# SyncE's list: a weight load that gave way to a transpose looks again from its new place

## The chip, the cores and the metric

The kernel runs on one core of one Trainium2 chip. The metric is the device time of one execution in microseconds (us); shorter is better. The core has five engines that run side by side: TensorE (PE in the profile), VectorE (DVE), ScalarE (ACT), GpSimd (POOL) and SyncE (SP). SyncE computes nothing here; it issues every transfer of the kernel, loads as well as transposes, one after the other in the order of one fixed list.

## The reference

Four residual layers on a sequence of 2048 rows of 576 numbers in bf16: attention, MLP, attention, MLP, with the same two sets of weights used twice.

```python
def _A_ref(x, wqkv, wo):                       # 32 heads of 18, window W = 256
    qkv = (x @ wqkv).reshape(B, S, 3, H, Dh)...
    scores = einsum("bhqd,bhkd->bhqk", q, k) * (Dh ** -0.5)
    mask = (idx[:, None] - idx[None, :] >= 0) & (idx[:, None] - idx[None, :] < W)
    p = softmax(where(mask, scores, -1e9))
    o = einsum("bhqk,bhkd->bhqd", p, v)
    return o... @ wo
def _B_ref(x, w1, b1, w2, b2):                 # 576 -> 4608 -> 576
    y = _layernorm(x)
    h = gelu(einsum("bsd,df->bsf", y, w1) + b1)
    return einsum("bsf,fd->bsd", h, w2) + b2
x = A_x
x = x + _A_ref(_layernorm(x), A_wqkv, A_wo)
x = x + _B_ref(_layernorm(x), B_w1, B_b1, B_w2, B_b2)
x = x + _A_ref(_layernorm(x), A_wqkv, A_wo)
x = x + _B_ref(_layernorm(x), B_w1, B_b1, B_w2, B_b2)
```

## The kernel before

**Tiles and chunks.** The rows are cut into 16 tiles of 128, and four tiles make a chunk of 512 rows. With two layers there are eight chunks, k = 0 to 7. The attention of chunk k runs interleaved with the MLP of chunk k - 1, so that TensorE has matmuls while ScalarE does exponentials.

**Stages.** Each task carries the name of its stage. For the attention of chunk k: `q{k}` makes queries, keys and values (matmuls at L855, for chunk 1 at L799), `ea{k}`, `eb{k}`, `ec{k}` are scores, exponentials, masks and the product with the values (L922, L933, L954, L975), `t{k}` is the output projection with its residual, statistics and normalization (L796, L1031, L711, L736). For the MLP: `ga`, `gb`, `gc` are the three thirds of the first matmul with its Gelu (L1088, L1098), and `ma`, `mb`, `mc` the three thirds of the second (L796 and L799, residual at L1031). `ln{k}` normalizes the rows for the queries of chunk k.

**Transposes.** Matmuls need their inputs with the contracted dimension on the partitions. So normalized rows `xn` are transposed by a transfer into `xnTa` (for the attention) or `xnTm` (for the MLP), at L759, and queries and keys `qn` into `qT` and `kT`, at L895. Both are issued by SyncE. Before an `xn` tile is transposed, GpSimd copies its last 64 columns (L744). For odd chunks each transpose into `xnTm` also names the buffers `kx0` and `kx1` as written, so that it waits for the one before it to land.

**Weight loads.** The weights of the MLP do not stay in the on-chip memory; they are streamed from HBM for each chunk. `w1` comes in six blocks per chunk into three slots; one block is three transfers, one of 768 KB and two of 48 KB. Two blocks are asked for in each of `ga`, `gb` and `gc`, always for a stage later on. `w2` comes in thirds into one buffer of two halves, two transfers of 864 KB each. All are issued at L648 (`dma`) and appear as `w_sb<-in_B_w_dram`; a load waits until the matmuls that read the buffer's old content are done. In the task's field `dma` they are "w1" and "w2", and a transpose is "t".

**The planner.** `Plan.schedule` plays the whole program through with an estimated cost for each task. It repeatedly takes the task that can start earliest, with priorities and nudges by stage as tie-breaks. The result, `order`, is the list of tasks with planned start times `st`, and each engine executes its part of the list in that order; the order is fixed when the kernel is built, and what each task waits for is worked out from what it reads and writes. A task's `ready` is the planned time at which its data are there.

**The pass that the change touches.** After the plan is made, a last pass shifts some weight loads back in the list. `turns` holds the planned start and the ready time of every transpose. A load of w1 or w2 that is planned at `st` gets the new place `at`, just behind the last transpose that starts less than 4 us after `st` and has its data at most `YIELD` = 3 us after `st`. Only loads planned from `YIELD_FROM` on are looked at. Whatever depends on a load is kept behind it through `first`. Then the list is sorted by the new places.

Of the kernel before, what the change touches and what calls it, by code (L numbers as in the profile page):

```python
# [186 lines left out]
class Plan:  # L187
# [75 lines left out]
    def schedule(self):  # L263
# [58 lines left out]
        while len(order) < n:  # L322
            best = None
            cands = []
            for e in ENGS:
                for t in released[e]:
                    st = max(free[e], t.ready)
                    if t.port:
                        st = max(st, port)
                    got = ()  # L330
                    if t.alloc:
# [3 lines left out]
                        st = max(st, when)  # L335
# [6 lines left out]
            _, t, st, got = best  # L342
            if t.eng == "pe" and t.fifo is None and st < self.feed_until and starves(t, st, got):
                for c in sorted(cands, key=lambda c: c[0]):
                    if c[2] < self.feed_until and (c[1].fifo is not None or not starves(*c[1:])):
                        _, t, st, got = c
# [19 lines left out]
            if t.dma is not None:  # L366
# [3 lines left out]
                while over > 0 and q:  # L370
                    a, b, d = q[0]
# [3 lines left out]
                    else:  # L375
                        a = b
# [4 lines left out]
                at = max(served.get(t.eng, 0.0), st + t.cost + min(t.lat, 2.0))  # L381
# [27 lines left out]
        turns = [(st, t.ready) for st, t in order if t.dma == "t"]  # L409
        first = {}  # L410
        for st, t in order:
            at = max(st, first.get(id(t), 0.0))
            if st >= YIELD_FROM and t.dma in ("w1", "w2"):
                at = max([at] + [a + 0.0001 for a, ready in turns if st < a < st + 4.0 and ready <= st + YIELD])
            first[id(t)] = at
            for s, _ in t.succ:
                first[id(s)] = max(first.get(id(s), 0.0), at + 0.0001)
# [3 lines left out]
        for st, t in order + [(0.0, None)]:  # L421
# [5 lines left out]
            at = [i for i, x in enumerate(run) if x.wide is None]  # L427
# [17 lines left out]
TURN_DMA = 0.8  # L445
TURN_FROM = 40.0
YIELD = 3.0
YIELD_FROM = 100.0
WARM_UNTIL = 140.0
FEED_UNTIL = 40.0  # L450

# [877 lines left out]
```

## Time and profile before

| | |
|---|---|
| three runs, median (lowest to highest) | 867.01 us (866.78 to 867.51) |
| the profiled execution, total | 866.17 us |
| the profiled execution, span | 864.5 us |
| granted TensorE clock | 1.0 of full speed |
| busy share of the span | TensorE 98%, ScalarE 68%, VectorE 46%, GpSimd 44% |
| moved by DMA | 119.81 MB, 139 GB/s on average |
| transfers issued by SyncE for w1 and w2 into `w_sb` | 190 (46 of 864 KB, 48 of 768 KB, 96 of 48 KB) |
| transposes: `xnTm`, `qT`, `xnTa`, `kT` | 32, 28, 28, 26 |

The span is the time from the first to the last recorded instruction; the total adds what lies around it. In the views a row of a timeline gives the start in us, the duration in us, the engine, the line and the operation with its tile, then the number of instructions that were merged, and in brackets the idle time before it with what ended it. `SPq` is SyncE's queue: the duration there is that of the issue, not of the transfer. A row of the waits gives who waited for whom, the us in total, how often, and the longest.

### The profile page before, as it was taken

Reading aid. Unit: us, or ns where it says so; the run is one execution under the profiler, and the core shown is the slowest. Engines: PE = TensorE matmul, PEld = TensorE weight load, DVE = VectorE, ACT = ScalarE, POOL = GpSimd, SP = SyncE. Lnnn points to the kernel's source line nnn. Section 1 sums busy time; section 2 is a strip of 40 time slices with the busy share of each in tenths; the row PEclk is TensorE's granted clock in tenths of the full one; section 3 lists DMA queues with packets and bytes.
Section 4 is the critical chain, followed back from the end, with each engine's and each line's share of the span. In section 5 each row is a group of like instructions: output and inputs, shape, how many; then the busy total and the mean of one; then the engine's idle time right before and its main releaser. Section 6 shows DMA issues by size and latency. Waiting matters only on the chain.

```text
span 864.5 us, 27552 instructions
## 1 busy us (share of the span) xinstructions
PE 848.6 (98%) x11875; PEld 523.3 (61%) x11875; DVE 394.7 (46%) x934; ACT 591.7 (68%) x723; POOL 380.1 (44%) x568
## 2 busy tenths in 40 slices
PE   8899999999999999989999999999999999999998
PEld 6555556656657665565665655656556556556656
DVE  6779323644328443374434832665234424243012
ACT  4986788788577697556674878628787689871730
POOL 3777544476135662264430853425454276222100
DMA  7995634553475723857356454584526854555320
GB/s 187 188 155 98 217 124 109 147 156 76 140 179 107 168 94 122 189 98 196 97 143 190 101 129 135 85 169 127 170 87 140 211 157 128 182 165 144 121 84 28
DMA packets 181866, 119.81 MB, mean 139 GB/s; under 512 B 107441, under 2 KB 181745, under 8 KB 181745
## 3 DMA queue, kind: packets, MB, share of 16 engines
q1 hardware_dynamic: 181744, 118.05, 54.6%
q8 instruction: 94, 1.54, 0.8%
q14 instruction: 28, 0.22, 0.1%
HBM read 90.10 MB, written 2.36 MB: 107 GB/s over the span
## 4 chain that ended last, share of the span: by engine, by line
PE 88%; DMA 5%; DVE 4%; POOL 1%; issue 1%; ACT 1%; SPq 0%; POOLq 0%; DVEq 0%
PE ps L1088 32%; PE ps L796 26%; PE ps L799 10%; PE ps L855 8%; PE ps L922 6%; PE ps L975 5%; DMA xnTm<-xn 2%; PE ps L815 1%; DMA x_res<-in_A_x_dram 1%; DVE x_res L1031 1%; POOL pT L954 1%; DVE st_all L711 1%; DMA kT<-qn 1%; ACT pT L933 1%; DVE qn L876 1%
## 5 line engine op out<-in xcount | busy, mean ns | idle before, releaser
L954 POOL TENSOR_SCALAR_AFFINE_SELECT pT<-pT 128x512 bf16<-128x512 bf16 (+2 forms) x376 | 285.0, 781 | 271.4 <-ACT pT L933 265.8
L933 ACT ACTIVATE pT<-ps 128x1024 bf16<-128x1024 f32 (+2 forms) x366 | 343.8, 1013 | 77.1 <-PE ps L922 76.7
L1088 PE MATMUL ps<-xnTm,w_sb 64*128 64x512 bf16 x2592 | 288.2, 376 | 2.5 <-DVE mv_all L715 1.2
L1098 ACT ACTIVATE hT<-ps,b1col 128x512 bf16<-128x512 f32 x276 | 167.3, 687 | 156.7 <-PE ps L1088 156.3
L1088 PEld LDWEIGHTS ps<-xnTm,w_sb 64*128 64x128 bf16 x2592 | 128.8, 94 | 147.2 <-issue 8.9
L796 PE MATMUL ps<-w_sb,hT 128*128 128x288 bf16 x1458 | 193.5, 287 | 0.0
L1031 DVE TENSOR_TENSOR x_res<-ps,x_res 128x288 f32<-128x288 f32 x224 | 100.1, 450 | 159.5 <-PE ps L796 143.0
L796 PEld LDWEIGHTS ps<-w_sb,hT 128*128 128x128 bf16 x1458 | 136.0, 98 | 49.5 <-issue 13.3
L984 DVE STREAM_TRANSPOSE oq<-ps 128x512 f32<-128x512 f32 x64 | 45.7, 713 | 124.9 <-PE ps L975 124.4
L876 DVE CAST qn<-ps 128x288 bf16<-128x288 f32 x120 | 49.1, 449 | 102.4 <-PE ps L855 95.5
L799 PE MATMUL ps<-w_sb,hT 128*32 128x288 bf16 x2616 | 91.4, 286 | 0.8 <-issue 0.7
L855 PE MATMUL ps<-wqkv,xnTa 64*128 64x288 bf16 x1296 | 89.7, 283 | 1.4 <-DVE vA L863 0.7
L855 PEld LDWEIGHTS ps<-wqkv,xnTa 64*128 64x128 bf16 x1296 | 61.9, 94 | 28.3 <-PE ps L855 3.6
L799 PEld LDWEIGHTS ps<-w_sb,hT 128*32 128x32 bf16 x2616 | 67.5, 97 | 14.6 <-issue 4.9
L922 PE MATMUL ps<-qT,kT 32*128 32x128 bf16 (+2 forms) x1280 | 62.5, 270 | 3.7 <-DMA kT<-qn 2.8
L711 DVE BATCH_NORM_STATS2 st_all<-x_res 128x6 f32<-128x288 f32 (+1 forms) x128 | 53.6, 443 | 4.5 <-DMA x_res<-in_A_x_dram 3.7
L1104 POOL TENSOR_TENSOR x_res<-x_res,b2bc 128x576 f32<-128x576 f32 x32 | 40.5, 1286 | 29.9 <-ACT hT L1098 29.8
L975 PE MATMUL ps<-pT,vA 128*20 128x384 bf16 (+2 forms) x1472 | 50.3, 271 | 0.0
L724 POOL TENSOR_SCALAR vtmp<-mv_all 128x1 f32<-128x1 f32 (+1 forms) x43 | 8.8, 204 | 92.2 <-DVE mv_all L715 88.2
L863 DVE CAST vA<-ps 128x288 bf16<-128x288 f32 x64 | 26.6, 448 | 46.0 <-PE ps L855 44.2
L922 PEld LDWEIGHTS ps<-qT,kT 32*128 32x128 bf16 x1280 | 19.1, 92 | 42.6 <-issue 23.9
L796 PE MATMUL ps<-wo_sb,attT 128*128 128x288 bf16 x320 | 41.6, 286 | 0.3 <-DVE b1col L1211 0.3
(56 smaller groups left out, 472.0 us busy)
## 6 DMA issues: line engine op xcount, KB each, us to landing
w_sb<-in_B_w_dram SPq DMA_DIRECT2D x46, 864.0 KB, 5.8
w_sb<-in_B_w_dram SPq DMA_DIRECT2D x48, 768.0 KB, 4.9
w_sb<-in_B_w_dram SPq DMA_DIRECT2D x96, 48.0 KB, 4.6
wqkv<-in_A_wqkv_dram SPq DMA_DIRECT2D x3, 576.0 KB, 5.4
x_res<-in_A_x_dram SPq DMA_DIRECT2D x3, 576.0 KB, 5.0
out_dram<-x_res SPq DMA_DIRECT2D x12, 144.0 KB, 2.1
wqkv<-in_B_w_dram SPq DMA_DIRECT2D x2, 864.0 KB, 5.1
wo_sb<-in_A_wo_dram SPq DMA_DIRECT2D x4, 144.0 KB, 4.1
```

Of the source, the lines that this page charges most:

```text
L711: add("dve", lambda e, i=i, s=s: e.bn_stats(st_all[:, t, i, :], s[:, t, i * HB:(i + 1) * HB]), reads=res, writes=[f"st{t}_{i}"], cost=0.37 ...
L796: return e.matmul(bank(b)[:, 0:HB], lhs, rhs, start=start, stop=stop, skip_group_check=True)
L799: ins = e.matmul(bank(b)[32 * j:32 * j + 32, 0:HB], lhs[:, 32 * j:32 * j + 32], rhs, start=start, stop=stop, tile_position=(0, 32 * j), sk ...
L855: ins = e.matmul(bank(bs[o])[:, 0:HB], xnTa[r:r + 64, c, i * 128:(i + 1) * 128], wqkv[r:r + 64, c, col:col + HB], start=(c == 4), stop=(ph ...
L876: add("dve", lambda e, b=bs[o], dst=dst: e.tensor_copy(dst, heads_of(bank(b))), reads=[bs[o]], writes=[f"qn{sl}h{o}"], cost=0.375, lat=0.1 ...
L922: ins = e.matmul(two(bs[j // 2])[:, j % 2, col:col + nq * 128], k_of(T0 + so)[0][32 * j:32 * j + 32, g, :], qs[32 * j:32 * j + 32, g, qo * ...
L933: add("act", lambda e, h2=h2: e.activation(pT[:, sl, 2 * h2:2 * h2 + 2, lo:hi], two(bs[h2])[:, :, lo:hi], ACT.Exp, scale=SCALE), reads=[bs ...
L954: add("pool", lambda e, ap=ap, pat=pat, sgn=sgn, kind=kind: e.affine_select(ap, ap, pattern=pat, compare_op=(ALU.is_ge if kind == "d" else ...
L975: ins = e.matmul(bank(bo)[32 * j:32 * j + VW, qo * 128:(qo + nq) * 128], vA[:, (T0 + so) % VS, 8 * j + g, :], pT[:, sl, j, col:col + nq * ...
L1031: add("dve", lambda e: e.tensor_tensor(x_res[:, t, sl], bank(b)[:, 0:HB], x_old[:, t, sl], ALU.add), reads=[b] + ([f"xin{t}"] if first els ...
L1088: ins = e.matmul(bank(bks[i])[:, 0:n], w1_sb[r:r + 64, sls[i], col:col + 128], xnTm[r:r + 64, k % 2, c, 0:n], start=(c == 4), stop=(ph == ...
L1098: add("act", lambda e, ff=ff, hd=hd, bk=bk: e.activation(hd[:, 0:n], bank(bk)[:, 0:n], ACT.Gelu_apprx_tanh, bias=b1col[:, ff:ff + 1]), rea ...
```

## The change

The look is put into a loop. A load begins at its own place `at`; as long as there is a transpose that starts less than 4 us after `at`, has its data at most 3 us after `at`, and starts less than 6 us after the load's planned `st`, `at` goes just behind it and the look is repeated from there. The old window began at `st` and was used once. The pass also begins with loads planned at 70 us instead of 100.

```diff
@@ -411,7 +411,10 @@
         for st, t in order:
             at = max(st, first.get(id(t), 0.0))
             if st >= YIELD_FROM and t.dma in ("w1", "w2"):
-                at = max([at] + [a + 0.0001 for a, ready in turns if st < a < st + 4.0 and ready <= st + YIELD])
+                more = True
+                while more:
+                    more = [a + 0.0001 for a, ready in turns if at < a < at + 4.0 and ready <= at + YIELD and a < st + 6.0]
+                    at = max([at] + more)
             first[id(t)] = at
             for s, _ in t.succ:
                 first[id(s)] = max(first.get(id(s), 0.0), at + 0.0001)
@@ -445,7 +448,7 @@
 TURN_DMA = 0.8
 TURN_FROM = 40.0
 YIELD = 3.0
-YIELD_FROM = 100.0
+YIELD_FROM = 70.0
 WARM_UNTIL = 140.0
 FEED_UNTIL = 40.0
```

## The prediction

> **What bounds the kernel now.** I read the page's busy times first, then the table of waits for TensorE, then the chain that ended last.
>
> ```profile
> span 864.5 us, 27552 instructions
> PE 848.6 (98%) x11875; PEld 523.3 (61%) x11875; DVE 394.7 (46%) x934; ACT 591.7 (68%) x723; POOL 380.1 (44%) x568
> ...
> PE ps L922 <- DMA kT<-qn: 2.8, 1, 2.8
> ...
> PE ps L1088 <- DMA xnTm<-xn: 0.9, 2, 0.5
> ...
> PE ps L799 <- DMA xnTa<-xn: 0.7, 1, 0.7
> ```
>
> TensorE is busy for 848.6 of 864.5 us. The change moves only transfers, so all it can win lies in the 16 us in which TensorE is idle. In the table of waits the longest single wait of TensorE is one of 2.8 us, of the scores (L922) for a transposed key tile. No row of that table names a weight tile: no matmul was seen waiting for a load. So a load may land later at no cost as long as it keeps a cover, and a transpose that lands earlier is worth something only at one of these waits.
>
> The chain places that wait, and SyncE's timeline and the DMA issues of the same stretch show what stood around it (the last number of an issue row is the us from the start of the issue to the landing):
>
> ```profile
> 369.51 7.23 DMA kT<-qn
> 376.74 0.05 issue
> 376.79 0.35 PE ps L922 x12
> ...
> 367.55 1.24 SPq L895 DMA_TRANSPOSE qT<-qn  x1
> 368.89 0.53 SPq L648 DMA_DIRECT2D w_sb<-in_B_w_dram  x1
> 369.51 1.24 SPq L895 DMA_TRANSPOSE kT<-qn  x1
> 370.81 1.33 SPq L648 DMA_DIRECT2D w_sb<-in_B_w_dram  x2
> ...
> w_sb<-in_B_w_dram SPq DMA_DIRECT2D x1, 768.0 KB, 5.3
> qT<-qn SPq DMA_TRANSPOSE x1, 3.1
> kT<-qn SPq DMA_TRANSPOSE x1, 7.2
> ```
>
> The key transpose at 369.51 was issued right behind a 768 KB weight load and took 7.2 us to land; the query transpose just before the load took 3.1. TensorE went idle until the slow one had landed.
>
> **Which steps the change moves.** For this the planner's own list for the kernel before is enough; its times serve here for the order alone. A load of w1 or w2 already gives way to transposes planned within 4 us after it whose data are ready within 3. The new loop repeats the look from the place so reached, up to 6 us after the load's own start. At the wait above the list has the load at 363.06, the query transpose at 365.70 and the key transpose at 367.00 with its data at 366.45. The old look stops at 363.06 + 3 = 366.06 and leaves the key transpose behind the load; the new one starts again at 365.70, reaches 368.70, and takes it. Going through the list in the same way, six loads move, each behind one more transpose: this one (w1, stage gc2.2); the first w1 load of ga1.1 behind an xnTa transpose; the first w2 load of mb1 behind a qT transpose; both w2 loads of mc1 behind an xnTa transpose; and the last, 48 KB load of ga4.1 behind an xnTa transpose. The lower YIELD_FROM moves nothing: the loads planned from 70 to 100 lie at 85 to 99, and the next transpose in the list comes at 137. No other engine's order changes, and no wait is added.
>
> **The key transpose, the one place that pays.** TensorE's and VectorE's rows there, and two rows for landings of key transposes, the pair at 659.76 having no load ahead:
>
> ```profile
> 366.70 1.55 DVE L876 CAST qn<-ps 128x288 bf16<-128x288 f32 x4 [11.80 <-PE ps L855]
> 373.25 0.78 PE L796 MATMUL ps<-wo_sb,attT 128*128 128x288 bf16 x5
> 376.79 0.35 PE L922 MATMUL ps<-qT,kT 32*128 32x128 bf16 x12 [2.77 <-DMA kT<-qn]
> ...
> 659.76 2.62 SPq L895 DMA_TRANSPOSE kT<-qn  x2
> kT<-qn SPq DMA_TRANSPOSE x2, 3.2
> DMA to landing us min/median/max: 3.0/3.9/7.2
> ```
>
> The casts that feed the key transpose end at 366.70 + 1.55 = 368.25, and the query transpose's issue ends at 367.55 + 1.24 = 368.79. So the key transpose can take the load's place at 368.89, 0.62 earlier, with no load ahead of it. What it then takes to land is not in this trace, only bounded: 3.0 at the fastest key transpose, 7.2 at the slowest. I take 3.2 to 3.9, the pair without a load and the median over all, since the pair is the nearest row: a transpose directly behind a transpose. It lands at 372.1 to 372.8. TensorE's work before the gap ends at 373.25 + 0.78 = 374.03, so 1.2 to 1.9 us are to spare and the whole 2.77 goes. At the slow end, 368.89 + 7.2 = 376.1, only 0.7 goes.
>
> What becomes late next, with 2.77 taken off? The rows that follow the gap:
>
> ```profile
> 373.86 1.70 SPq L759 DMA_TRANSPOSE xnTm<-xn  x1
> xnTm<-xn SPq DMA_TRANSPOSE x1, 3.7
> ...
> 375.17 0.56 DVE L736 TENSOR_SCALAR xn<-x_res,mv_all,rstd 128x576 bf16<-128x576 f32 x1
> 377.89 0.46 DVE L1031 TENSOR_TENSOR x_res<-ps,x_res 128x288 f32<-128x288 f32 x1 [2.16 <-PE ps L796]
> 378.77 1.56 POOL L954 TENSOR_SCALAR_AFFINE_SELECT pT<-pT 128x1536 bf16<-128x1536 bf16 x1 [3.64 <-ACT pT L933]
> 380.27 0.24 POOL L744 COPY xn<-xn 128x64 bf16<-128x64 bf16 x1
> 380.58 1.20 SPq L759 DMA_TRANSPOSE xnTm<-xn  x1
> 386.96 1.20 SPq L759 DMA_TRANSPOSE xnTm<-xn  x1
> xnTm<-xn SPq DMA_TRANSPOSE x1, 2.5
> 390.07 0.39 PE L1088 MATMUL ps<-xnTm,w_sb 64*128 64x512 bf16 x2
> ```
>
> The next matmul stage (L1088 at 390.07) reads four xnTm transposes, and each of these waits for the landing of the one before (they write the same two extra names). The second waits for GpSimd's copy, which stands behind a mask, which waits for the exponentials of the delayed scores: this chain moves forward with TensorE, from 380.58 to 377.81. The first transpose, which does not move, lands at 373.86 + 3.7 = 377.56, 0.25 sooner. The bytes queued ahead of it stay the same. The last lands at 386.96 + 2.5 = 389.46, 0.6 before its matmul, and that spare is kept. VectorE could use 377.89 - 2.77 = 375.12 for the residual but works until 375.73: 0.6 us late, which lands in the idle 2.16 that this row shows, and in four PSUM banks ahead of TensorE. Against this I book 0.05 for the issue after the wait. Term: **-2.7 us**, bounds -0.7 and -2.8.
>
> The load itself is now issued at about 368.89 + 1.24 + 0.1 = 370.2, 1.3 later, and by its 5.3 lands at about 375.5. The tiles that it brings are block 20 of the weights (chunk 3, third block), which stage gb3 reads first:
>
> ```profile
> 425.37 11.66 PE ps L1088 x108
> ...
> 376.80:864.50 487.70, 483.12 (x6437) 298.07 (x6437) 198.47 (x453) 315.83 (x388) 188.30 (x273) 1.00 0.51 134
> ```
>
> That is 50 us later, so the cost is nothing. In the stretch after the gap (window, length, then busy time of TensorE first) TensorE is busy for 483.12 of 487.70 us; every load and transpose there waits for data or buffers that TensorE's own progress frees, so the rest of the program slides forward as a block and nothing in it is tied to an absolute time.
>
> **The other four places.** SyncE's rows at three of them, and two first uses of the moved loads:
>
> ```profile
> 189.15 0.53 SPq L648 DMA_DIRECT2D w_sb<-in_B_w_dram  x1
> 247.01 0.58 SPq L648 DMA_DIRECT2D w_sb<-in_B_w_dram  x1
> w_sb<-in_B_w_dram SPq DMA_DIRECT2D x1, 864.0 KB, 5.6
> 262.96 3.67 PE ps L799 x120
> 286.61 1.12 SPq L648 DMA_DIRECT2D w_sb<-in_B_w_dram  x2
> 304.20 2.21 PE ps L799 x72
> ```
>
> No wait of TensorE for a qT or xnTa transpose lies in these stretches, so the transposes that come forward win nothing; a moved load loses one transpose's issue, about 1.3 us. The tightest cover is at 247.01: 247.01 + 1.3 + 5.6 = 253.9 against the first use at 262.96, 9 us. At 286.61 the pair's first use is at 304.20, 17.6 us behind. The transpose that stays behind the moved loads has the same bytes ahead of it in either order. Term: 0, bounds -0.3 and +0.3.
>
> A rule of the Trainium skill speaks against moving loads back: "DMA: Bandwidth & Descriptors", section Rules for kernel authors, says to issue a transfer early and to wait for it late. It prices nothing here; followed strictly it would leave all six loads where they are and the sum at 0.
>
> **The sum** is -2.7 + 0 = -2.7 us. The profiled execution took 866.17 (span 864.5 and 1.7 around it), which becomes 863.5. The median of the three runs, 867.01, lies 0.84 above the profiled one; the same -2.7 gives **864.3 us**.
>
> **The rivals.**
>
> The key transpose stays late although the load is gone from ahead of it: two transposes in a row hold each other up. For it: the slow one stood behind another transpose as well as behind the load. Against it: the pair at 659.76 landed in 3.2. At 7.2 from the new place 0.7 goes: 866.3. Chance 0.08.
>
> The Trainium skill, "DMA: Bandwidth & Descriptors", section Queues, rings and completion order, says that each DMA engine takes descriptors in ring order, yet that a later transfer may finish writing before an earlier one. If the second half ruled here, the load would not have been what held the key transpose; the 3.1 and the 7.2 on the two sides of the load speak for the first half.
>
> The gap closes but TensorE waits again at the next stage: the four xnTm transposes do not come forward, because the first lands more than 0.25 + 0.6 later than before. Then L1088 still starts at about 390 and the time stays at 867.0. For it: the spare is short. Against it: the bytes ahead are unchanged. Chance 0.06.
>
> Slower: a moved load arrives after its matmul. The place would be the w2 load at 247.01, with 9 us of cover. It begins to cost when the transpose now ahead of it holds SyncE for more than 9 us beyond the 1.3; to end slower than before by 0.2% it must also eat the 2.7, so it needs about 13.4 us, and then the time is 868.8. Against it: no transpose near these places occupied SyncE for half of that. With it I count loads that collide elsewhere in a way that these rows do not show. Chance 0.07.
>
> That the change moves none of the six is excluded by the list, and is not priced.
>
> **How the numbers follow.** The forecast has 0.79; its own range, with 0.3 for the terms and 0.4 for the scatter of the runs, is 863.6 to 865.0. The rival with 0.7 us reaches to 866.3, and with it 863.6 to 866.3 leaves out less than 2 in 10. About 0.2%, 1.7 us, is what a measurement of this kernel can tell from no change. Faster by more: the forecast, 0.79. Within: the first two rivals, 0.14. Slower: 0.07.
>
> **What would show it.** In the changed profile SyncE issues qT, kT and then the load near 367.6 to 370.2; the key transpose lands in under 5 us; the wait of L922 for kT is gone from TensorE's table, and L1088 of that stage starts at about 387.3 instead of 390.07. The prediction is wrong if TensorE still has a wait of more than 1 us between 374 and 388, or if any row has TensorE waiting for a weight load.

## The result and the profile after

The changed kernel takes 864.54 us (median of 6 runs, 863.44 to 865.17) against 867.62 us (6 runs) for the kernel before: ratio 0.996, 95% interval 0.9947 to 0.9974, which is 2.3 to 4.6 us. The forecast was 864.3 with 863.6 to 866.3. The profiled execution took 864.44 us with a span of 862.7. In the profile after, lines from the edit on stand three lines lower: the scores L922 are L925, the MLP's first matmul L1088 is L1091, the load L648 is L651.

The table of waits for TensorE (who waited for whom, us in total, times, longest) has no row for `kT` any more:

```profile
span 862.7 us, 27552 instructions
...
PE ps L818 <- DMA wqkv<-in_A_wqkv_dram: 2.3, 3, 1.4
PE ps L892 <- DVE qn L879: 1.1, 1, 1.1
PE ps L1091 <- DVE vA L866: 1.1, 1, 1.1
```

Its longest rows now belong to the first 120 us. The first of them, at the very start, is a wait for the attention's weights (wqkv), one that the profile before does not have. By its letter this is one of the prediction's signs of being wrong (any row of TensorE waiting for a weight load). But no load of the start is touched by the change, and the profile of experiment 3, whose start is that of the kernel before, has such a wait of 1.8 us too: it differs from one execution to the next. So two spans taken as a whole compare two starts as well (864.5 and 862.7, only 1.8 apart), and the place itself has to be read by differences. SyncE's and TensorE's timelines and the issues with their us to landing, at the place of the swap:

```profile
369.01 1.24 SPq L898 DMA_TRANSPOSE qT<-qn  x1
370.35 1.27 SPq L898 DMA_TRANSPOSE kT<-qn  x1
371.71 1.76 SPq L651 DMA_DIRECT2D w_sb<-in_B_w_dram  x3
375.33 11.86 SPq L762 DMA_TRANSPOSE xnTm<-xn  x4
...
374.70 0.78 PE L799 MATMUL ps<-wo_sb,attT 128*128 128x288 bf16 x5
375.43 0.35 PE L925 MATMUL ps<-qT,kT 32*128 32x128 bf16 x12
388.78 3.41 PE L1091 MATMUL ps<-xnTm,w_sb 64*128 64x512 bf16 x30
...
qT<-qn SPq DMA_TRANSPOSE x1, 3.3
kT<-qn SPq DMA_TRANSPOSE x1, 4.9
xnTm<-xn SPq DMA_TRANSPOSE x1, 2.8
```

The key transpose now stands between the query transpose and the loads. TensorE reaches the last matmuls before the old gap at 374.70, 1.45 later than in the profile before (373.25); it reaches the next MLP stage at 388.78, 1.29 earlier (390.07). The place alone therefore gave 1.45 + 1.29 = 2.74 us, which is the whole wait of 2.77.

### The profile page after: what moved, and what is told of

Read it like the earlier page. It is cut to its first block, busy times and chain, and to the rows that moved or that the text cites. A ratio compares the mean times of both kernels' runs of the same rounds, so it can differ in the third digit from the quotient of the medians.

```text
span 862.7 us, 27552 instructions
## 1 busy us (share of the span) xinstructions
PE 847.9 (98%) x11875; PEld 524.8 (61%) x11875; DVE 394.5 (46%) x934; ACT 591.9 (69%) x723; POOL 380.8 (44%) x568
## 4 chain that ended last, share of the span: by engine, by line
PE 89%; DMA 4%; DVE 3%; issue 1%; POOL 1%; ACT 1%; SPq 1%; POOLq 0%; DVEq 0%
PE ps L1091 32%; PE ps L799 28%; PE ps L802 10%; PE ps L858 8%; PE ps L925 6%; PE ps L978 5%; DMA xnTm<-xn 1%; DMA x_res<-in_A_x_dram 1%; PE ps L818 1%; ACT pT L936 1%; POOL pT L957 1%; SPq L651 1%; DMA wqkv<-in_A_wqkv_dram 1%; DVE x_res L1034 1%; DVE st_all L714 1%
## 5 line engine op out<-in xcount | busy, mean ns | idle before, releaser
L1091 PE MATMUL ps<-xnTm,w_sb 64*128 64x512 bf16 x2592 | 288.3, 376 | 1.9 <-DVE vA L866 1.1
L1091 PEld LDWEIGHTS ps<-xnTm,w_sb 64*128 64x128 bf16 x2592 | 130.8, 94 | 144.9 <-issue 8.5
L925 PE MATMUL ps<-qT,kT 32*128 32x128 bf16 (+2 forms) x1280 | 62.5, 270 | 0.9 <-ACT pT L936 0.6
L925 PEld LDWEIGHTS ps<-qT,kT 32*128 32x128 bf16 x1280 | 19.1, 92 | 40.1 <-issue 24.3
```

The source lines that it names most:

```text
L925: ins = e.matmul(two(bs[j // 2])[:, j % 2, col:col + nq * 128], k_of(T0 + so)[0][32 * j:32 * j + 32, g, :], qs[32 * j:32 * j + 32, g, qo * ...
L1091: ins = e.matmul(bank(bks[i])[:, 0:n], w1_sb[r:r + 64, sls[i], col:col + 128], xnTm[r:r + 64, k % 2, c, 0:n], start=(c == 4), stop=(ph == ...
```

## The experiments

Each ratio is against the kernel before, run on the same chip with it. The diffs are shortened; three dots stand for text left out. An edit shifts the lines behind it, so the scores are L922, L923, L925 or L927, depending on the kernel.

**1. The key transpose alone.** From the changed kernel, only the load of stage gc2.2 uses the new loop, and YIELD_FROM is back at 100:

```diff
+                if t.stage != "gc2.2+":
+                    at = max([at] + [... old rule ...])
+                more = t.stage == "gc2.2+"
                 while more:
```

> Of the six moved loads only the 768 KB w1 load of stage gc2.2 is moved behind the key transpose; the other five stay as before. Theory (this one swap is the whole gain): TensorE's 2.8 us wait for the key transpose is gone, and the time falls by 2.8 us (2.3 to 3.3), ratio about 0.9968, the same as with the whole change. Rival (the other four places bring a part): the fall is under 2.3 us. Rival (any reordering shifts the time by chance): no fall that an interval can show.

Measured: 864.59 us against 867.93, ratio 0.9949 (0.9936 to 0.9961). The wait for `kT` is gone; what is left around the place is a short wait for `qT`, which in this execution took 4.6 us to land (the kernel's waits, then its issues):

```profile
PE ps L927 <- DMA qT<-qn: 0.7, 1, 0.7
...
qT<-qn SPq DMA_TRANSPOSE x1, 4.6
kT<-qn SPq DMA_TRANSPOSE x1, 4.2
```

This one swap gives as much as the whole change. The interval, 3.4 to 5.6 us, begins above the 2.8 that the profile's wait accounts for; the two medians are 3.3 apart. The granted clock that is on record for each run tells where a part of the excess lies. Of the 26 runs of the kernel before, 15 have a mean below 1.0 of full speed (0.996 or 0.998, median 868.7 us) and 11 have 1.0 (median 866.7); all 6 runs of this kernel have 1.0. So 2.1 us remain between runs at the full clock, and 1.2 go with falls of the clock, of which the profile of before has none.

**2. The other five loads alone.** From the changed kernel:

```diff
+                if t.stage == "gc2.2+":
+                    at = max([at] + [... old rule ...])
+                more = t.stage != "gc2.2+"
                 while more:
```

> The other five loads are moved, the load of gc2.2 stays ahead of the key transpose. Theory: TensorE still waits 2.8 us for the key transpose and the time is that of before within 0.3 us, ratio 1.000. Rival (the other places bring a part): a fall of 0.5 us or more. Rival (a moved load or the transpose left behind it lands too late): a rise, and a new wait of TensorE for a weight or an xnTa tile between 187 and 305 us or between 500 and 530 us.

Measured: 868.03 us against 867.93, ratio 0.9999 (0.9985 to 1.0012). The other places bring or cost nothing that the interval can show (1.3 us faster to 1.0 slower). At the swap the wait is back, 2.5 us in all, this time split between the two transposes, because the query transpose also landed late (4.8 us) and took a part of it:

```profile
PE ps L927 <- DMA kT<-qn: 1.6, 1, 1.6
PE ps L927 <- DMA qT<-qn: 0.9, 1, 0.9
...
qT<-qn SPq DMA_TRANSPOSE x1, 4.8
```

The second edit of the change, YIELD_FROM, does nothing: with 70 or 100 the new loop gives the same list on every engine.

**3. More ahead of the key transpose.** From the kernel before, all three loads of the block stand ahead of it:

```diff
-                at = max([at] + [... if st < a < st + 4.0 and ready <= st + YIELD])
+                at = max([at] + [... if st < a < st + 4.0 and ready <= st + YIELD
+                                 and (t.stage != "gc2.2+" or a < 366.0)])
```

> From the kernel before: the key transpose is put behind all three loads of the block (768 KB and twice 48 KB) instead of behind the first only, so the suspected cause is made larger. Theory (what stands ahead of it in SyncE's list and in the transfer queue holds it): it is issued 1.3 us later, the two issues, and has 96 KB more ahead, 0.3 us; TensorE waits 4.2 to 4.5 us instead of 2.8, and the time rises by 1.5 us, ratio 1.0017. Rival (the query transpose just ahead was what held it): with two more issues between them it lands 3.1 to 3.9 after its issue, TensorE waits about 0.8 us, and the time falls by 2 us.

Measured: 867.58 us against 867.93, ratio 0.9989 (0.9976 to 1.0003), with TensorE waiting 2.19 us. Both expectations missed. SyncE's timeline, TensorE's and the issues:

```profile
368.43 1.24 SPq L895 DMA_TRANSPOSE qT<-qn  x1
369.77 1.74 SPq L648 DMA_DIRECT2D w_sb<-in_B_w_dram  x3
371.61 1.26 SPq L895 DMA_TRANSPOSE kT<-qn  x1
...
377.09 0.35 PE L922 MATMUL ps<-qT,kT 32*128 32x128 bf16 x12 [2.19 <-DMA kT<-qn]
...
qT<-qn SPq DMA_TRANSPOSE x1, 3.1
kT<-qn SPq DMA_TRANSPOSE x1, 5.4
```

Counted from the start of the load's issue, the transpose lands after 371.61 - 369.77 + 5.4 = 7.2 us here and after 369.51 - 368.89 + 7.2 = 7.8 us in the kernel before. Issued 1.2 us later, it landed no later. The profile of experiment 2 gives a third case, with the same 768 KB ahead:

```profile
370.76 1.99 SPq L653 DMA_DIRECT2D w_sb<-in_B_w_dram  x1
372.84 1.24 SPq L900 DMA_TRANSPOSE kT<-qn  x1
...
kT<-qn SPq DMA_TRANSPOSE x1, 5.6
```

That is 372.84 - 370.76 + 5.6 = 7.7 us from the start of the load's issue. So in these three profiles the place in SyncE's list is not itself a price: the issues run while the big load is still being moved (it landed 5.3 to 6.5 us after its issue), and the transpose lands 7.2 to 7.8 us after the load's issue whether it is issued 0.6, 1.8 or 2.1 us behind it. My 1.3 us for two more issues should have been nothing. The rival also fails: with the load between them the transpose did not land in 3.1 to 3.9.

**4. Fewer bytes ahead.** From the kernel before, with its order:

```diff
-        dma("sp", w1_sb[:, sl, 0:4 * GW]... c=4), B_w1[0:512, cols]... 
+        nc_ = 1 if B == 20 else 4
+        dma("sp", w1_sb[:, sl, 0:nc_ * GW]... c=nc_), B_w1[0:128 * nc_, cols]... 
```

> From the kernel before, with its order: the w1 load of gc2.2 that stands ahead of the key transpose brings 192 KB instead of 768 (the other three quarters of that block keep old weights; one block of one chunk is computed with them). Theory (the load's bytes hold the transpose): 576 KB less at the 320 to 390 GB/s that the queue moves there are 1.5 to 1.8 us; the transpose lands about 5.5 us after its issue instead of 7.2, TensorE's wait falls to 1.0 to 1.3 us, and the time falls by 1.6 us, ratio 0.998. Rival (a fixed cost of changing from transpose to load and back): the transpose still lands about 7 us after its issue, the wait stays above 2.3 us, and the time stays.

Measured: 864.45 us against 867.93, ratio 0.9963 (0.9945 to 0.998).

```profile
PE ps L923 <- DMA kT<-qn: 1.1, 1, 1.1
...
w_sb<-in_B_w_dram SPq DMA_DIRECT2D x1, 192.0 KB, 3.5
kT<-qn SPq DMA_TRANSPOSE x1, 5.6
```

The transpose lands 1.6 us sooner after its issue and the wait falls by 1.7, as the bytes say: 576 KB in 1.6 us is 369 GB/s. At that rate, an estimate, the remaining 192 KB hold it for another 0.5 us, which leaves 5.1 us for the transpose with no load ahead; the changed kernel has 4.9. The time fell by more than the expected 1.6 us: the interval, 1.7 to 4.8 us, begins just above it. Here too the clock takes part: 1 of these 7 runs has a mean below 1.0, against 15 of the 26 of the kernel before. The Trainium skill, "DMA: Bandwidth & Descriptors", section Queues, rings and completion order, has each DMA engine take descriptors in ring order; experiments 3 and 4 agree with that half. Its other half, that a later descriptor may finish its write before an earlier one, does not show here: in the profiles at this place the transfers land in the order of their issue.

**5. The changed kernel again**, as the yardstick for experiments 6 and 8.

> The changed kernel once more, as the yardstick for the two kernels that are built from it. Every theory: about 3 us under the kernel before, ratio 0.9965, with no wait of TensorE for a key transpose.

Measured: 864.53 us against 868.38, ratio 0.9962 (0.9946 to 0.9978). The key transpose took 5.1 us to land, and there is no wait for it.

**6. Fewer bytes behind.** The edit of experiment 4 on the changed kernel.

> From the changed kernel, with its order: the w1 load that now follows the key transpose brings 192 KB instead of 768 (one block of one chunk is computed with old weights in three of its four quarters). The key transpose of the changed kernel landed 4.9 us after its issue where the prediction took 3.2 to 3.9. Theory A (the load behind it takes part of the transfer engines while the transpose is still moving): it lands in 3.2 to 4.0 us. Theory B (the query transpose ahead of it is what it waits for): it still lands in 4.7 to 5.1. The time stays within 0.3 us of the changed kernel by both, since the transpose has landed before TensorE asks for it.

Measured: 865.34 us against 868.38, ratio 0.9962 (0.9948 to 0.9977). That is 0.8 us over experiment 5, outside the expected 0.3, though the two groups of runs overlap. The key transpose landed in 4.8 us:

```profile
kT<-qn SPq DMA_TRANSPOSE x1, 4.8
```

So the bytes of the load behind it are not why it takes nearly 5. Since a small load also stood behind it, the next run took all of them away.

**7. Nothing behind.** The three loads go behind the four `xnTm` transposes that follow:

```diff
+            if t.stage == "gc2.2+":
+                at = 381.83
             first[id(t)] = at
```

> From the changed kernel: all three loads of the block of gc2.2 are moved away, behind the four xnTm transposes that follow (planned cover until stage gb3 remains), so the key transpose has the query transpose just ahead and nothing behind it. With a quarter of the load's bytes behind it, it still landed 4.8 us after its issue. Theory A (any load behind it slows it, whatever its size): it lands in 3.1 to 3.6 us, as the pair of key transposes near 660 us did. Theory B (the query transpose ahead is what it waits for): it still lands in 4.7 to 5.1. The time stays within 0.5 us of the changed kernel by both.

Measured: 863.96 us against 867.23, ratio 0.9965 (0.995 to 0.9981).

```profile
368.54 1.24 SPq L900 DMA_TRANSPOSE qT<-qn  x1
369.88 2.41 SPq L900 DMA_TRANSPOSE kT<-qn  x1
...
371.00:372.00 1.00, 1.00 (x11) 0.80 (x9) 1.00 (x5) 0.00 (x0) 1.00 (x2) 1.00 0.09 12
372.00:373.00 1.00, 0.49 (x4) 0.16 (x2) 0.90 (x4) 0.00 (x0) 0.85 (x3) 1.00 1.24 267
...
qT<-qn SPq DMA_TRANSPOSE x1, 4.6
kT<-qn SPq DMA_TRANSPOSE x1, 4.2
```

Neither theory: the key transpose took 4.2 us, the query transpose ahead of it 4.6. In the window from 371 to 372 (last two columns: share of the DMA engines, GB/s) hardly anything moves, 12 GB/s, with both in flight and no load near. What holds such a pair for about a microsecond stays open. It is not the load behind, and it is not peculiar to this pair (see below).

**8. How much a load may be late.** From the changed kernel, the first w2 load of mb1 goes about 12 us further back:

```diff
+            if t.stage == "mb1+" and "w2s0" in t.writes:
+                at = 255.74
             first[id(t)] = at
```

> From the changed kernel: the first w2 load of stage mb1, issued at 249.8 us there, is moved further back, behind five more transposes and three loads, to about 261.7. It measures the cover that the prediction gave this load (about 9 us beyond the change). Theory (the cover ends where the first matmul reads the tile, 264.2 us in the changed kernel): the load lands 5.6 to 6.4 us after its issue, at 267.3 to 268.1, TensorE waits 2.3 to 3.9 us for it, and the time rises by as much over the changed kernel. Rival (the cover is larger, other waits are there already): no wait for a weight tile and no rise. Rival (a late load costs more than its wait, since it pushes the transposes behind it): a rise of over 5 us.

Measured: 870.15 us against 868.38, ratio 1.0031 (1.0017 to 1.0045), 5.6 us over the yardstick of experiment 5. The chain, TensorE's waits and groups, and windows by time (seventh number: TensorE's granted clock):

```profile
263.74 5.59 DMA w_sb<-in_B_w_dram
...
269.37 5.18 PE L804 MATMUL ps<-w_sb,hT 128*32 128x288 bf16 x120 [3.81 <-DMA w_sb<-in_B_w_dram]
...
L804 PE MATMUL ps<-w_sb,hT 128*32 128x288 bf16 x120 | 5.2, 347 | 3.8 <-DMA w_sb<-in_B_w_dram 3.8
...
269.37:270.37 1.00, 1.00 (x20) 0.69 (x24) 0.00 (x0) 0.00 (x0) 0.00 (x0) 0.50 1.18 299
271.37:272.37 1.00, 1.00 (x28) 0.72 (x24) 0.00 (x0) 0.00 (x0) 0.00 (x0) 0.62 0.88 295
272.37:273.37 1.00, 1.00 (x40) 0.84 (x36) 0.96 (x2) 0.00 (x0) 0.00 (x0) 1.00 0.08 16
```

and the same 120 matmuls in the changed kernel:

```profile
264.16 3.85 PE L802 MATMUL ps<-w_sb,hT 128*32 128x288 bf16 x120
```

The wait itself, 3.81 us, is at the top of what the cover gave. The rise is over 5 us, as the rival had it, but not by the rival's cause, the transposes pushed back: the matmuls after the wait ran at first with the granted clock at 0.50 and took 5.18 us instead of 3.85. The wait and these 1.33 us are 5.1 of the 5.6. Of the 10 runs, 9 have a mean clock below 1.0; the profiled one, with this one fall, has 0.998.

## Why the prediction was right

**Where it pays.** Shown: one swap gives the whole gain (experiment 1), the other five loads nothing (2), the lower YIELD_FROM nothing. The wait of 2.8 us in the table of before was the right row to start from.

**The size.** The sum, -2.7 us, is this wait alone, in one profile at the full clock. Between runs at the full clock the swap gave less, 2.1 us in experiment 1 and 2.4 in experiment 5 (866.9 against 864.5); between all runs it gave more, 3.1 us, along with fewer runs in which the clock fell, for which the sum has no term. That the forecast lies 0.2 us from the measured median is in part luck.

**What held the transpose.** The load's bytes, as argued (3 and 4); the 0.62 us of a better place in SyncE's list, which the prediction counted as part of it, is worth nothing by itself while the load's transfer is under way (3).

**The landing was mis-sized.** The prediction took 3.2 to 3.9 us, from a pair of key transposes near 660 us, and saw 1.2 to 1.9 us to spare. It landed in 4.2 to 5.1 us in six profiles. In the changed kernel that is 370.35 + 4.9 = 375.25, and TensorE's work before it ends at 374.70 + 0.78 = 375.48: 0.2 us to spare; in experiment 5 it is 368.44 + 5.1 = 373.54 against 372.80 + 0.78 = 373.58, next to none. The wait went as a whole all the same, which is luck as far as the prediction goes: it counted on over 1 us. The pair near 660 was the exception and not the nearest row. The trace of before has others without a load ahead, for instance a key transpose directly behind a query transpose:

```profile
555.06 1.23 SPq L895 DMA_TRANSPOSE qT<-qn  x1
556.35 2.18 SPq L895 DMA_TRANSPOSE kT<-qn  x1
...
kT<-qn SPq DMA_TRANSPOSE x1, 4.2
```

The key transposes issued directly behind another transpose at 344.97, 575.57 and 667.04 took 4.8, 4.1 and 4.7 us. So the rival of two transposes that hold each other up, put at 0.08, was half right: the key transpose stayed slow in such a pair, but by too little to bring the wait back.

**What becomes late next.** Right: L1091 follows without a wait, the first `xnTm` transpose landed in 2.8 us rather than the 3.7 that it took before, and the rest slid forward. The forecast start of 387.3 became 388.78 since this execution reached the place 1.45 us later.

**The cover of the late loads.** The tightest was put at 9 us beyond the change, and experiment 8 bears that out: a landing takes 5.59 us, and a wait of 3.81 begins when the load starts at 263.74, so it could have started at 259.9. In that execution its old neighbour in the list started at 251.1, so 8.8 us were free. The price beyond the cover was too low: this wait came with a fall of the clock, which added 1.3 us to its length.

## What to carry to other kernels

A transposed tile that is needed at once should not queue behind a large load that is needed much later; look for the wait in the table of the bound engine, and follow the late transfer back to what was issued just ahead of it. What such a transfer cost those behind it was here its bytes, not its place in the issuing engine's list. Of the six moves that the rule made here, only the one that ended a wait of the bound engine counted; the rest needed no more than enough cover. For the landing of a transfer in its new place, take the slow rows of its kind as well as the fast ones.

## What the hardware showed that I had not expected

The granted TensorE clock fell to 0.50 after an idle time of 3.81 us and came back to 1.00 about 3 us later, while it stayed at 1.00 after the idle time of 2.77 us in the kernel before:

```profile
374.03:376.79 2.76, 0.00 (x0) 0.00 (x1) 1.70 (x5) 0.00 (x0) 1.10 (x2) 1.00 1.27 135
376.79:378.79 2.00, 2.00 (x26) 1.56 (x27) 0.74 (x2) 1.51 (x2) 0.02 (x1) 1.00 0.12 19
```

The Trainium skill, "TensorE: Matmul & The Clock Gate", section What's actually happening, puts the clock at half after an idle window of about 3.4 us and back at full after as long a busy one; both rows agree. The trace of experiment 2 does not fit it as a rule for a single wait. There the clock was at 0.50 from 51.30 to 54.50 at least, and TensorE's longest wait just before was one of 1.81 us (TensorE's row and windows; the seventh number is the clock):

```profile
49.79 0.79 PE L801 MATMUL ps<-wqkv,xnTa 128*128 128x288 bf16 x5 [1.81 <-DVE qn L881]
...
49.79:51.10 1.31, 1.31 (x25) 0.73 (x29) 1.25 (x4) 0.14 (x1) 1.26 (x2) 1.00 1.28 201
51.30:54.50 3.20, 3.20 (x41) 1.65 (x34) 1.73 (x4) 2.60 (x4) 1.23 (x2) 0.50 1.04 88
54.70:56.00 1.30, 1.30 (x29) 0.76 (x29) 1.07 (x3) 1.00 (x2) 0.50 (x1) 1.00 1.03 193
```

So no length of a wait that is safe can be read from these traces. The runs show how often the clock fell. In the experiments 31 of the 54 runs of the kernel before have a mean clock below 1.0; of the 32 runs of kernels with the key transpose ahead of the load (the changed kernel twice, experiments 1, 6 and 7) only 2 have. The falls thus seem to go with the wait for the key transpose, and to be a part of what the swap gains; but no profile shows one at that place, so this is likely and not shown.
